# Moving two input loads and a weight load, with a new order of all work, in a linear-attention and mixer-MLP kernel

## The chip, the cores and the metric

The kernel runs on one core of one Trainium2 chip. A core has five engines that run side by side, each through its own list in order: TensorE (PE) multiplies, VectorE (DVE), ScalarE (ACT) and GpSimd (POOL) do element-wise work, and SyncE (SP) issues the DMAs here, apart from a few that ScalarE issues at the start. The metric is the time of one execution on the device in microseconds (us); less is better.

## The reference, cut to what matters

S = 2048 tokens of width D = 448; H = 16 heads of 28; MLP width 1792; all arrays are bf16.

```python
xn = layernorm(A_x)
# A: linear attention
q, k, v = heads(xn @ wqkv)
phi = lambda t: concat(softmax(t @ w_phi), softmax(-t @ w_phi))
kv, z = sum_s phi(k)^T v, sum_s phi(k)
A = (phi(q) kv / (phi(q) z + 1e-6)) @ wo
# B: token mixer and MLP, on xn
h  = gelu(layernorm(xn) @ w1)
x1 = xn + shift(h) @ w2        # four column blocks, shifted by +1, -1, +2, -2 tokens
B  = x1 + gelu(layernorm(x1) @ w3) @ w4
out = A_x + A + B
```

## The kernel before, in words

The tokens are cut into 16 tiles of 128. Every instruction is first recorded by a small class (`Recorder`, lines 19 to 222) together with the memory that it reads and writes; `solve` works out from the recorded order which instruction has to wait for which, and `emit` writes each engine's list. So the order in which the Python code calls things fixes two matters: the order within each engine's own list, SyncE's DMA issues among them, and who waits for whom. An instruction that waits holds up all that is behind it on its engine. Nearly all rows of a profile therefore carry the line of a helper: 204 a matmul, 208 a transpose on PE, 212 a ScalarE instruction, 216 one of VectorE or GpSimd, 219 a DMA transpose, 222 a plain DMA.

The loads at the start (lines 366 to 387) alternate between SyncE's queue and ScalarE's. `load_x(i, n)` brings n tiles of x into `xtok`; `load_half` brings half a weight. `load_wT` (line 381) transposes 112 rows' worth of the q (t = 0) or k (t = 1) weights by DMA into `wT`, whose memory is called `hi` in a profile; five such transposes are recorded before the order of the work begins. `load_w2` (line 389) loads w2 in three DMAs: 336 KB for three row blocks, and the last 64 rows twice, once for each half of the partitions.

The work comes in two lists, written out by hand.

The first list (lines 944 to 968) is handed to `chain` (line 561) and holds the jobs until the first products with w2. PE's rows are used in two halves, a lower and an upper one of 64 rows each, which run side by side; `chain` interleaves the steps of the two halves and holds the upper half of a product back by a lag of 400 columns. A string of digits says for each product which half takes four of its seven steps. The jobs are:

- `L(("m", i))`: the layer-norm statistics of tile i, two VectorE instructions. `L(("r", i, 1))`: the inverse root on GpSimd; `L(("q", i, 1))`: the same on ScalarE. `L(("a", i))`: normalise tile i into `xn` on VectorE; `L(("p", i))`: the same on GpSimd, behind a small negation.
- `XT(i, bank, n, engine)`: transpose n tiles on PE and copy them from PSUM to `xnT` on ScalarE, on VectorE or half on each ("2"). `XD(i)`: transpose tile i by a DMA.
- `ZV(i, EV(...))`: the V product of tile i (weight `wv`), and the engine that copies it out into `vaug`. `vb` and `gb` name the PSUM banks.
- `ZW`, `ZH`: the products with w1 for a group of four tiles, or half a group, and their GELU on ScalarE into `hT`. `ZR(h, bank)`: those for the last 64 columns of w1; their GELU goes to `hR`, and `rest_T(h)` transposes that by DMA into `hRT`. (In a profile hR has the name gT.)
- `FO`: folds the feature-map weights `w_phi` into the k or q weights (`wpk`, `wpq`). `phi_blocks` builds what the folds multiply with.
- `h_shift(g)`: six DMAs from `hT` to `hT` that move token columns for half of the tokens.
- `HD(bank, n)`: filler products on constants, whose result is not used.
- `HF(p, half)`: the halves of the first pair of k, w2 and q products; `HF(1, 0)` is the first one that reads w2, `hT` and `hRT`.

The second list (lines 1035 to 1059) holds the rest: k and q products and their exponentials (`k0`, `k1`, `q0`, `q1`), w2 products (`w0`, `w1_`), the k normalisation (`kn` on VectorE, `kx` on GpSimd), statistics of the second norm (`lo`), its scale (`sc`) and its application (`A` on GpSimd, `AD` on VectorE), DMA transposes (`T` of phi(q), `G` of the second norm's result), the sum over tokens (`K`), the w3 products (`a`, `b`), the attention output (`N`), the w4 and wo products (`f`) and the stores (`S`).

The name `w` in a profile stands for several tensors whose names are one letter and a digit, w1, w2, w3 and w4 among them.

Of the kernel before, what the change touches and what calls it, by code (L numbers as in the profile page):

```python
# [224 lines left out]
def bass_parallel_sum__linear_kernel_hedgehog__mixer_s_mlp__prompt_kernel(  # L225
    nc, A_x, A_wqkv, A_w_phi, A_wo, B_x, B_w1, B_w2, B_w3, B_w4, out,
):
    _, S, D = A_x.shape
# [14 lines left out]
    with es:  # L243
# [106 lines left out]
        def load_x(i, n, eng="SP"):  # L350
            R.dma(xtok[:, i:i + n, :], x2d[128 * i:128 * (i + n), :].rearrange("(j p) d -> p j d", p=128), eng)
# [9 lines left out]
        def load_half(dst, src, h, eng="SP"):  # L361
            R.dma(dst[:, 2 * h:2 * h + 2, :], src[192 * h:192 * h + 256, :].rearrange("(c p) d -> p c d", p=128), eng)
# [573 lines left out]
        def HF(p, n):  # L936
# [157 lines left out]
```

## Time and profile before

| | us |
|---|---|
| median of 3 runs | 171.0 (170.87 to 171.48) |
| the profiled execution | 171.11 |
| its span, from the first to the last instruction on the core | 169.4 |
| PE busy | 165.0 |
| VectorE busy | 109.9 |
| GpSimd busy | 92.4 |
| ScalarE busy | 79.6 |

The profile is one execution; its clock columns show TensorE granted its full clock (1.00) throughout. A matmul of a half-height tile overlaps one of the other half, so busy time of PE is not yet PE at its peak. "SPq" is SyncE's queue: a row there is the time that the issue of a DMA took, not its transfer. In a row of the timeline, the numbers are start and length in us, and a bracket at the end is the idle time of the engine before it, with what ended it. In a row of the groups, the numbers behind the bar are busy us and the mean in ns, and behind the second bar idle us. In a row of the DMA issues, the last number is the time from issue to landing.

### The profile page before, as it was taken

The page shows a single profiled execution, that of the slowest core. Times are in us where ns is not written, and L with a number is a line of the kernel's source. Part 1 is how long each engine was busy: PE and PEld are TensorE (multiplying, and loading weights), DVE is VectorE, ACT ScalarE, POOL GpSimd, SP SyncE. Part 2 cuts the span into 40 slices and gives each one's busy share as a digit, 9 for nine tenths or more (in the row PEclk, how much of TensorE's full clock was granted, in tenths as well). Part 3 has the DMA queues.
Part 4 walks back from the last instruction along what each step waited for, and adds up shares of the span by engine and source line. Part 5 has one row for each costly group of instructions (what it writes and reads, how often), then busy time and mean ns, then how long its engine had stood idle before and what let it go on. Part 6 is the DMA issues. An engine that isn't in the chain of part 4 may idle for free.

```text
span 169.4 us, 5416 instructions
## 1 busy us (share of the span) xinstructions
PE 165.0 (97%) x2355; PEld 99.2 (59%) x2355; DVE 109.9 (65%) x247; ACT 79.6 (47%) x107; POOL 92.4 (55%) x126
## 2 busy tenths in 40 slices
PE   8899999999999999999999999999999999999994
PEld 7476678666888775535554555545555555544453
DVE  2899777269999999995885836755755252560031
ACT  3489964849998787455242420440140222224000
POOL 5569872002999999994455684162362724252040
DMA  5995443799999976459785159363133112013021
GB/s 146 356 217 105 75 90 85 144 294 270 194 117 240 241 102 191 68 112 130 165 110 107 24 108 154 77 106 63 32 66 85 35 54 62 0 31 99 17 81 54
DMA packets 50583, 19.93 MB, mean 118 GB/s; under 512 B 41728, under 2 KB 49856, under 8 KB 50560
## 3 DMA queue, kind: packets, MB, share of 16 engines
q1 hardware_dynamic: 49440, 18.71, 55.1%
q10 hardware_dynamic: 1120, 0.89, 1.6%
q8 instruction: 18, 0.29, 0.8%
q14 instruction: 5, 0.04, 0.1%
HBM read 7.14 MB, written 1.84 MB: 53 GB/s over the span
## 4 chain that ended last, share of the span: by engine, by line
PE 86%; SPq 4%; DMA 4%; DVE 3%; POOL 1%; issue 1%
PE banks L204 85%; SPq L222 4%; DMA xtok<-in_A_x_dram 2%; DMA hRT<-gT 2%; DVE st L216 1%; PE banks L208 1%; DVE vaug L216 1%; POOL rs L216 1%; DVE mv L216 0%; POOL xn L216 0%; DVE xn L216 0%; SPq L219 0%
## 5 line engine op out<-in xcount | busy, mean ns | idle before, releaser
L212 ACT ACTIVATE phik<-banks 128x1024 bf16<-128x1024 f32 (+1 forms) x44 | 41.6, 987 | 63.5 <-PE banks L204 63.5
L204 PE MATMUL banks<-gT,w 64*128 64x512 bf16 x392 | 47.1, 376 | 0.1
L216 DVE TENSOR_TENSOR vaug<-banks,vaug 128x464 f32<-128x464 f32 (+3 forms) x65 | 32.8, 514 | 20.5 <-PE banks L204 18.8
L204 PE MATMUL banks<-w,phik 64*128 64x448 bf16 (+3 forms) x434 | 45.2, 343 | 0.0
L216 POOL TENSOR_TENSOR xnT<-vaug 128x280 bf16<-128x280 f32 (+1 forms) x32 | 18.1, 588 | 35.6 <-DVE vaug L216 35.6
L721 POOL TENSOR_TENSOR phik<-phik,rks 128x1792 bf16<-128x1792 bf16 x8 | 25.6, 3215 | 15.3 <-DVE rks L216 15.3
L204 PEld LDWEIGHTS banks<-w,phik 64*128 64x128 bf16 (+1 forms) x434 | 22.3, 94 | 19.5 <-issue 0.4
L204 PE MATMUL banks<-wv,xnT 64*128 64x448 bf16 (+2 forms) x222 | 33.0, 346 | 0.1
L204 PEld LDWEIGHTS banks<-gT,w 64*128 64x128 bf16 x392 | 18.3, 94 | 19.5 <-ACT phik L212 1.4
L216 POOL TENSOR_TENSOR vaug<-xn,xtok 128x448 f32<-128x448 bf16 x16 | 16.2, 1032 | 9.1 <-DVE vaug L216 9.1
L204 PEld LDWEIGHTS banks<-wv,xnT 64*128 64x128 bf16 (+1 forms) x222 | 13.7, 94 | 9.0 <-ACT xnT L212 0.8
L216 DVE RECIPROCAL vaug<-banks 128x16 f32<-128x16 f32 x16 | 4.1, 257 | 21.6 <-PE banks L204 21.6
L204 PE MATMUL banks<-xnT,w 64*128 64x512 bf16 (+1 forms) x105 | 17.6, 334 | 0.0
L216 DVE TENSOR_REDUCE ksum<-phik 128x64 f32<-128x1792 bf16 x8 | 16.0, 1997 | 0.2 <-ACT phik L212 0.2
L204 PE MATMUL banks<-wpk,xnT 64*128 64x448 bf16 x112 | 15.4, 349 | 0.0
L204 PE MATMUL banks<-wpq,xnT 64*128 64x448 bf16 x112 | 15.1, 349 | 0.0
L212 ACT ACTIVATE hi<-banks 128x896 bf16<-128x896 f32 x16 | 13.9, 937 | 1.2 <-PE banks L204 1.2
L204 PE MATMUL banks<-w,hT 64*128 64x448 bf16 x96 | 14.0, 349 | 0.0
L216 POOL TENSOR_TENSOR rs<-mv,mhalf 128x1 f32<-128x1 f32 (+1 forms) x14 | 9.6, 690 | 2.6 <-DVE mv L216 2.4
L216 POOL TENSOR_SCALAR g_tok<-xn,rs 128x512 bf16<-128x512 bf16 x12 | 9.2, 775 | 2.9 <-DMA gT<-g_tok 2.6
L204 PEld LDWEIGHTS banks<-wpk,xnT 64*128 64x128 bf16 x112 | 8.7, 94 | 2.6 <-ACT phik L212 0.2
L216 DVE BATCH_NORM_STATS2 st<-xtok 128x6 f32<-128x448 bf16 x16 | 9.7, 604 | 0.7 <-DMA xtok<-in_A_x_dram 0.7
(63 smaller groups left out, 167.2 us busy)
## 6 DMA issues: line engine op xcount, KB each, us to landing
w<-in_B_w_dram SPq DMA_DIRECT2D x2, 896.0 KB, 5.5
out_dram<-vaug SPq DMA_DIRECT2D x15, 112.0 KB, 1.9
w<-in_B_w_dram SPq DMA_DIRECT2D x2, 784.0 KB, 5.6
xtok<-in_A_x_dram SPq DMA_DIRECT2D x2, 448.0 KB, 6.5
wv<-in_A_wo_dram SPq DMA_DIRECT2D x2, 224.0 KB, 3.7
xtok<-in_A_x_dram SPq DMA_DIRECT2D x3, 112.0 KB, 4.0
xtok<-in_A_x_dram ACTq DMA_DIRECT2D x3, 112.0 KB, 4.2
w<-in_B_w_dram SPq DMA_DIRECT2D x1, 336.0 KB, 4.3
```

Of the source, the lines that this page charges most:

```text
L204: self.op("PE", lambda e: e.matmul(out, lhsT, rhs, start=start, stop=stop, skip_group_check=True), [out], [lhsT, rhs], tile=self._tile(lhsT))
L208: self.op("PE", lambda e: e.transpose(out, in_, ident), [out], [in_, ident], tile=self._tile(in_))
L212: self.op("ACT", lambda e: e.activation(out, in_, func, **kw), [out], [in_] + aps)
L216: self.op(eng, lambda e: getattr(e, name)(out, *args, **kw), [out], aps)
L222: self.op(eng, lambda e: e.dma_start(out, in_), [out], [in_], dma=True)
L721: R.op(pool, lambda e: e.tensor_tensor(ph, ph, wide, op=ALU.mult), [ph], [ph, wide, *after])
```

## The change

Four things are changed. The loads of x for tiles 2 and 3 stand ahead of those of wv. `load_w2` takes a part: part 0 is the 336 KB DMA, part 1 one DMA that brings the last 64 rows to both halves of the partitions, from a source that is read twice (a leading dimension of 2 with step 0); part 0 stands behind the V product of tile 2 and ahead of the last three `load_wT`, part 1 ahead of `phi_blocks`. Both lists are put in a new order, with other engines for some applications, roots and copies, other banks for some products and another string of digits. The statistics of the first norm are all `m` jobs, on VectorE, on both sides. The first norm has nine tiles applied on GpSimd and seven on VectorE on both sides, ten roots on GpSimd and six on ScalarE.

```diff
         load_x(0, 1)
         load_x(1, 1, "ACT")
+        load_x(2, 1)
+        load_x(3, 1, "ACT")
         load_half(wv, wv_d, 0)
         load_half(wv, wv_d, 1, "ACT")
-        load_x(2, 1)
-        load_x(3, 1, "ACT")
...
-        def load_w2(eng="SP"):
-            R.dma(w2[:, 0:NH, :], B_w2[0:REST, :].rearrange("(m p) d -> p m d", p=128), eng)
-            for h in range(2):
-                R.dma(w2[64 * h:64 * h + 64, NH, :], B_w2[REST:D, :], eng)
+        def load_w2(h, eng="SP"):
+            if h:
+                tail = B_w2[REST:D, :]
+                R.dma(w2[:, NH, :], bass.AP(tail.tensor, tail.offset, [[0, 2], *tail.ap]), eng)
+            else:
+                R.dma(w2[:, 0:NH, :], B_w2[0:REST, :].rearrange("(m p) d -> p m d", p=128), eng)
...
-        vb = {0: 6, 1: 7, 2: 5, 3: 0, 4: 6, 5: 5, 6: 1, 7: 1, 8: 0, 9: 7, 10: 6, 11: 2, 12: 7, 13: 7, 14: 5, 15: 2}
-        gb = ((4, 2, 3), (7, 6, 4), (3, 0, 5), (0, 5, 6))
+        vb = {0: 6, 1: 7, 2: 5, 3: 0, 4: 6, 5: 5, 6: 0, 7: 1, 8: 0, 9: 7, 10: 2, 11: 3, 12: 7, 13: 7, 14: 5, 15: 2}
+        gb = ((4, 2, 3), (7, 6, 4), (6, 0, 5), (0, 5, 6))
         spin(30)
         chain([
-            HD(1, 3), HD(3, 3), do(load_wT, 0, (1, 2, 3)), HD(2, 3), L(("m", 1)), L(("q", 1, 1)), L(("m", 0)),
-            L(("q", 0, 1)), HD(3, 3), L(("a", 1)), L(("p", 0)), HD(5, 3), XT(1, 2, 1, "ACT"), HD(0, 3), L(("m", 2)),
-            L(("m", 3)), XT(0, 2, 1, "ACT"), L(("q", 3, 1)), L(("r", 2, 1)), L(("m", 4)), L(("a", 3)), L(("q", 4, 1)),
-            L(("m", 5)), ZV(1, EV(1, "ACT", 1)), ZV(0, EV(0, "ACT", 1)), L(("p", 2)), XT(2, 4, 1, "ACT"),
-            inside(1, ZH(1, 0), XT(3, 0, 1, "ACT")), L(("m", 7)), L(("r", 5, 1)), L(("a", 4)), L(("p", 5)),
-            L(("q", 7, 1)), L(("m", 6)), L(("r", 6, 1)), ZH(2, 0), L(("a", 7)), ZV(2, EV(2, "ACT", 1)),
-            inside(1, ZH(0, 0), XT(4, 0, 1, "ACT")), L(("p", 6)), inside(2, ZH(0, 1, EW(0, 0, 1)), XT(5, 6, 1, "2")),
-            L(("m", 15)), inside(1, ZH(2, 1), XT(7, 0, 1, "2")), L(("q", 15, 1)), L(("p", 15)),
-            ZV(4, EV(4, "ACT", 1)), L(("m", 14)), inside(2, ZH(1, 1, EW(0, 1, 2)), XT(6, 0, 1, "DVE")), L(("m", 12)),
-            ZV(5, EV(5, "ACT", 1)), L(("r", 14, 1)), L(("m", 13)), L(("p", 14)), ZV(6, EV(6, "ACT", 1)), L(("m", 11)),
-            ZW(1, 0, EW(1, 0, 1)), ZW(1, 1, EW(1, 1, 1)), ZW(1, 2, EW(1, 2, 1)), L(("m", 10)), L(("r", 13, 1)),
-            L(("r", 12, 1)), XT(14, 2, 2, "ACT"), L(("a", 12)), L(("r", 11, 1)), ZV(7, EV(7, "DVE", 1)), L(("a", 13)),
-            L(("m", 8)), L(("p", 11)), ZV(3, EV(3, "ACT", 1)), ZV(15, EV(15, "ACT", 1)), XT(12, 6, 1, "2"),
-            do(kv_picks), XT(13, 3, 1, "2"), do(phi_blocks), L(("r", 10, 1)), L(("r", 8, 1)), XD(11),
-            L(("a", 10)), XD(10), ZV(14, EV(14, "ACT", 1)), L(("m", 9)), L(("p", 8)), ZV(12, EV(12, "DVE", 1)),
-            ZW(3, 0, EW(3, 0, 1)), XT(8, 3, 1, "ACT"), FO(1, 2, 0), do(h_shift, 0), L(("r", 9, 1)),
-            ZW(3, 2, EW(3, 2, 1)), FO(1, 0, 0), FO(1, 2, 1), ZV(13, EV(13, "ACT", 1)), ZW(3, 1, EW(3, 1, 1)),
-            FO(1, 0, 1), L(("p", 9)), ZV(8, EV(8, "DVE", 1)),
+            L(("m", 1)), L(("r", 1, 1)), L(("m", 0)), HD(1, 3), L(("q", 0, 1)), HD(6, 3), L(("p", 0)), HD(1, 3),
+            L(("a", 1)), L(("m", 2)), HD(5, 3), XT(1, 0, 1, "ACT"), HD(4, 3), L(("q", 2, 1)), HD(4, 3), L(("m", 3)),
+            L(("m", 4)), XT(0, 2, 1, "ACT"), L(("m", 5)), L(("q", 3, 1)), L(("p", 2)), ZV(1, EV(1, "ACT", 1)),
+            L(("p", 3)), L(("q", 4, 1)), ZV(0, EV(0, "ACT", 1)), L(("r", 5, 1)), L(("a", 4)), L(("m", 7)),
+            XT(2, 4, 1, "ACT"), ZH(2, 0), inside(1, ZH(1, 0), XT(3, 0, 1, "2")), L(("q", 7, 1)),
+            ZV(2, EV(2, "ACT", 1)), do(load_w2, 0), L(("m", 6)), L(("p", 5)), inside(1, ZH(0, 0), XT(4, 0, 1, "ACT")),
+            L(("q", 6, 1)), L(("p", 6)), L(("a", 7)), inside(2, ZH(0, 1, EW(0, 0, 1)), XT(5, 6, 1, "2")),
+            inside(1, ZH(2, 1), XT(7, 0, 1, "ACT")), L(("m", 15)), do(load_wT, 0, (1, 2, 3)), ZV(4, EV(4, "ACT", 1)),
+            L(("m", 14)), inside(2, ZH(1, 1, EW(0, 1, 2)), XT(6, 0, 1, "DVE")), ZV(5, EV(5, "ACT", 1)),
+            ZV(3, EV(3, "ACT", 1)), L(("m", 10)), L(("r", 14, 1)), ZW(1, 0, EW(1, 0, 1)), L(("a", 14)),
+            ZW(1, 1, EW(1, 1, 1)), L(("r", 15, 1)), L(("p", 15)), L(("r", 10, 1)), L(("m", 12)), L(("m", 8)),
+            ZW(1, 2, EW(1, 2, 1)), L(("m", 13)), L(("r", 12, 1)), XT(14, 2, 2, "DVE"), ZV(7, EV(7, "ACT", 1)),
+            ZV(6, EV(6, "ACT", 1)), L(("r", 13, 1)), L(("a", 12)), L(("m", 11)), L(("p", 13)),
+            ZV(15, EV(15, "DVE", 1)), XT(12, 6, 1, "DVE"), L(("a", 10)), XT(13, 3, 1, "ACT"), do(load_w2, 1),
+            do(phi_blocks), L(("r", 11, 1)), ZV(14, EV(14, "ACT", 1)), ZV(12, EV(12, "ACT", 1)), XD(10), L(("a", 11)),
+            L(("r", 8, 1)), XD(11), L(("m", 9)), L(("p", 8)), do(kv_picks), ZW(3, 0, EW(3, 0, 1)), XT(8, 3, 1, "ACT"),
+            FO(1, 2, 0), ZW(3, 2, EW(3, 2, 1)), FO(1, 0, 0), FO(1, 2, 1), ZV(13, EV(13, "ACT", 1)),
+            ZW(3, 1, EW(3, 1, 1)), FO(1, 0, 1), ZV(8, EV(8, "DVE", 1)), L(("r", 9, 1)), L(("p", 9)),
             inside(3, ZR(0, 6, (rest_out, 0, 6), (rest_T, 0)), XT(9, 1, 1, "DVE")), FO(0, 0, 0), FO(0, 2, 0),
-            ZR(1, 7, (rest_out, 1, 7)), do(load_w2), FO(0, 0, 1), ZW(2, 2, EW(2, 2, 1)), ZW(2, 1, EW(2, 1, 1)),
-            FO(0, 2, 1), do(load_w3, 0), ZV(10, EV(10, "ACT", 1)), ZW(2, 0, EW(2, 0, 1)), do(rest_T, 1),
-            ZV(9, EV(9, "ACT", 1)), ZV(11, EV(11, "DVE", 1)), HF(1, 0), HF(0, 0), HF(2, 0), HF(1, 1), do(late_3), do(kv_ones),
-            HF(0, 1), HF(2, 1), do(h_shift, 1)], 400,
-            "100100110101110000101010011110100")
+            do(late_3), do(h_shift, 0), ZR(1, 7, (rest_out, 1, 7)), FO(0, 0, 1), do(kv_ones), ZW(2, 2, EW(2, 2, 1)),
+            ZW(2, 1, EW(2, 1, 1)), ZW(2, 0, EW(2, 0, 1)), FO(0, 2, 1), do(load_w3, 0), ZV(11, EV(11, "ACT", 1)),
+            ZV(9, EV(9, "DVE", 1)), ZV(10, EV(10, "ACT", 1)), HF(1, 0), do(rest_T, 1), HF(0, 0), do(h_shift, 1),
+            HF(2, 0), HF(1, 1), HF(0, 1), HF(2, 1)], 400,
+            "010101010101101100001010011111000")
...
         play([
-            (lo, 1), (load_w3, 1), (k0, 1), (w0, 2), (lo, 0), (kn, 0), (k1, 1), (q0, 1), (w1_, 2), (q1, 1), (T, 0),
-            (k0, 2), (q0, 2), (k1, 2), (q1, 2), (k0, 3), (q0, 3), (T, 1), (kn, 1), (T, 3), (k1, 3), (w0, 4), (q1, 3),
-            (kx, 0), (kn, 2), (T, 2), (kx, 1), (w1_, 4), (kn, 3), (k0, 4), (T, 5), (w0, 6), (k1, 4), (lo, 3), (kx, 2),
-            (q0, 4), (lo, 2), (w1_, 6), (q1, 4), (kn, 4), (k0, 5), (kx, 3), (k0, 6), (sc, 0), (k1, 5), (w0, 8),
-            (wo_in,), (q0, 5), (A, 0), (w1_, 8), (k1, 6), (T, 6), (AD, 1), (T, 4), (q0, 6), (kn, 5), (T, 7), (q1, 5),
-            (w0, 10), (load_w4, 0), (A, 3), (k0, 7), (A, 2), (w1_, 10), (q1, 6), (lo, 5), (lo, 6), (w0, 12), (k1, 7),
-            (q0, 7), (G, 0), (K, 0), (kx, 4), (K, 1), (G, 1), (kx, 5), (lo, 7), (lo, 4), (G, 2), (K, 3), (K, 4),
-            (G, 3), (sc, 4), (K, 6), (A, 7), (kn, 6), (K, 9), (q1, 7), (load_w4, 1), (A, 6), (A, 4), (w1_, 12),
-            (K, 8), (K, 5), (K, 7), (lo, 10), (A, 5), (K, 11), (K, 2), (kx, 6), (G, 4), (kn, 7), (G, 7), (K, 10),
-            (a, 0), (lo, 11), (kx, 7), (a, 1), (G, 6), (b, 0), (lo, 12), (b, 1), (w0, 14), (a, 2), (lo, 8), (a, 3),
-            (lo, 9), (b, 2), (G, 5), (b, 3), (sc, 8), (w1_, 14), (T, 15), (a, 4), (a, 5), (b, 4), (b, 5), (T, 12),
-            (lo, 14), (K, 13), (lo, 15), (T, 10), (K, 15), (K, 14), (T, 14), (K, 12), (a, 6), (a, 7), (A, 9), (b, 6),
...
+            (k0, 1), (lo, 1), (w0, 2), (k1, 1), (lo, 0), (kn, 0), (q0, 1), (w1_, 2), (q1, 1), (kx, 0), (kn, 1),
+            (k0, 2), (q0, 2), (k1, 2), (k0, 3), (q1, 2), (load_w3, 1), (kx, 1), (T, 0), (q0, 3), (k1, 3), (T, 1),
+            (kn, 2), (w0, 4), (q1, 3), (w1_, 4), (kn, 3), (kx, 2), (k0, 4), (w0, 6), (k1, 4), (lo, 2), (q0, 4),
+            (T, 2), (w1_, 6), (kx, 3), (wo_in,), (T, 4), (q1, 4), (k0, 5), (lo, 3), (sc, 0), (k0, 6), (kn, 4),
+            (k1, 5), (A, 0), (T, 5), (T, 3), (w0, 8), (q0, 5), (w1_, 8), (AD, 1), (k1, 6), (T, 7), (q0, 6), (q1, 5),
+            (A, 3), (w0, 10), (T, 6), (load_w4, 1), (A, 2), (k0, 7), (G, 0), (kn, 5), (kx, 4), (w1_, 10), (kx, 5),
+            (lo, 5), (q1, 6), (w0, 12), (k1, 7), (G, 3), (lo, 6), (q0, 7), (K, 0), (lo, 4), (lo, 7), (K, 9), (K, 1),
+            (K, 2), (sc, 4), (K, 5), (G, 2), (K, 3), (G, 1), (kn, 6), (A, 5), (q1, 7), (w1_, 12), (K, 6), (AD, 4),
+            (K, 8), (load_w4, 0), (K, 4), (K, 11), (A, 6), (A, 7), (lo, 9), (K, 10), (G, 6), (lo, 10), (K, 7),
+            (kx, 6), (a, 0), (a, 1), (b, 0), (b, 1), (w0, 14), (kn, 7), (a, 2), (a, 3), (lo, 8), (b, 2), (kx, 7),
+            (b, 3), (w1_, 14), (a, 4), (lo, 12), (lo, 11), (sc, 8), (a, 5), (b, 4), (lo, 13), (b, 5), (lo, 14),
+            (G, 5), (G, 7), (K, 12), (K, 14), (K, 13), (K, 15), (a, 6), (G, 4), (kc,), (a, 7), (kb,), (T, 9),
...
```

More of the change, by code (lines that the diff above doesn't have):

```diff
@@ new lines, in bass_parallel_sum__linear_kernel_hedgehog__mixer_s_mlp__prompt_kernel @@
+            (lo, 15), (T, 13), (A, 11), (b, 6), (b, 7), (N, 0), (T, 11), (f, 1, 0), (N, 1), (a, 9), (a, 8), (AD, 8),
+            (G, 8), (b, 9), (AD, 10), (N, 2), (b, 8), (f, 2, 0), (a, 11), (N, 3), (a, 10), (T, 12), (G, 10), (A, 9),
+            (G, 9), (f, 3, 0), (b, 10), (b, 11), (f, 4, 0), (G, 11), (N, 5), (a, 12), (sc, 12), (a, 13), (f, 1, 1),
+            (f, 3, 1), (S, 0), (b, 13), (A, 13), (N, 4), (f, 2, 1), (N, 7), (b, 12), (f, 4, 1), (T, 8), (a, 15),
+            (a, 14), (S, 2), (b, 15), (N, 6), (T, 10), (b, 14), (A, 12), (f, 1, 2), (AD, 14), (a, 16), (A, 15),
@@ new lines, in bass_parallel_sum__linear_kernel_hedgehog__mixer_s_mlp__prompt_kernel @@
+            (a, 17), (G, 14), (S, 1), (b, 16), (S, 3), (b, 17), (G, 13), (T, 15), (f, 3, 2), (a, 18), (N, 9), (G, 12),
+            (f, 2, 2), (N, 8), (b, 18), (a, 19), (G, 15), (f, 4, 2), (b, 19), (N, 11), (a, 20), (f, 1, 3), (f, 3, 3),
+            (b, 20), (N, 13), (f, 2, 3), (f, 4, 3), (S, 5), (a, 21), (S, 7), (a, 22), (T, 14), (b, 21), (N, 10),
+            (b, 22), (f, 1, 4), (f, 3, 4), (a, 23), (S, 4), (N, 12), (f, 2, 4), (a, 24), (S, 6), (f, 4, 4), (b, 24),
+            (b, 23), (N, 15), (f, 1, 5), (S, 8), (a, 25), (N, 14), (f, 3, 5), (b, 25), (f, 2, 5), (a, 26), (f, 4, 5),
@@ L1060, in bass_parallel_sum__linear_kernel_hedgehog__mixer_s_mlp__prompt_kernel @@
+            (a, 27), (S, 10), (S, 11), (S, 9), (b, 26), (b, 27), (f, 1, 6), (f, 2, 6), (fin_tails,), (f, 3, 6),
+            (S, 13), (S, 12)])
         fin_full(14)
```

12 lines of the change are left out of this document (removed).

## The prediction, made before the changed kernel was run

> **What bounds the kernel now.** I read the page's busy table first, then the busy time by stage, then the chain that ended last, and only then the single rows at the places where these three disagree.
>
> ```profile
> span 169.4 us, 5416 instructions
> PE 165.0 (97%) x2355; PEld 99.2 (59%) x2355; DVE 109.9 (65%) x247; ACT 79.6 (47%) x107; POOL 92.4 (55%) x126
> ```
>
> TensorE (PE) is busy 97% of the span. The change removes no matmul: six groups of filler products (HD), 30 spins, the same V, w1, fold and head products, two tiles (10, 11) by DMA transpose, all stand on both sides of the diff, and each V or w1 product has seven of its eight half-height steps whichever way its digit points. So the time can only move where PE waits, or runs one half of its rows alone. The stages (columns: PE, PEld, DVE, ACT, POOL busy with counts, clock, DMA share, GB/s) show where that is:
>
> ```profile
> 5.70:13.00 7.30, 6.46 (x123) 4.20 (x118) 6.72 (x20) 5.32 (x15) 5.48 (x10) 1.00 1.25 265
> 32.00:36.00 4.00, 3.77 (x40) 2.09 (x41) 0.85 (x5) 2.40 (x3) 0.00 (x0) 1.00 0.80 223
> ```
>
> PE idles 0.84 us in 5.7 to 13 and 0.23 us in 32 to 36; behind that the chain below shows next to nothing. Two places remain: the start, where it waits for normalised tiles, and the join at 33 us, where the first product with w2 begins. The chain, in order of time, names the join:
>
> ```profile
> 30.12 2.72 DMA hRT<-gT
> 32.97 32.65 PE banks L204 x513
> 65.72 101.35 PE banks L204 x1269
> ```
>
> After the transpose into hRT lands, at 32.84, PE runs to the end practically without a gap. Whatever PE gains before 33 us is therefore kept, if the other engines move with it; whatever it loses is lost.
>
> **The change, part by part.**
>
> *w2 out of the queue ahead of hRT.* SyncE's queue (start, length, operation, count; the colon rows give shortest, median and longest in ns) is full from 5.48 on:
>
> ```profile
> 5.48 14.00 SPq L219 DMA_TRANSPOSE hi<-in_A_wqkv_dram  x8
> L219 SPq DMA_TRANSPOSE hi<-in_A_wqkv_dram x8: 1247/1260/3019, 5.5 to 18.2; - x8
> 19.52 3.49 SPq L219 DMA_TRANSPOSE xnT<-xn  x2
> 23.06 4.55 SPq L222 DMA_DIRECT2D hT<-hT  x6
> 27.65 2.43 SPq L222 DMA_DIRECT2D w<-in_B_w_dram  x3
> 30.12 1.27 SPq L219 DMA_TRANSPOSE hRT<-gT  x1
> L222 SPq DMA_DIRECT2D w<-in_B_w_dram x5: 542/589/1204, 27.6 to 37.2; - x5
> PEld banks L204 <- DMA w<-in_B_w_dram: 0.3, 1, 0.3
> ```
>
> Three w2 issues stand between the shift copies (hT) and the hRT transpose: 30.12 - 27.65 = 2.47 us. Two issues come in their place, one ahead of the last three wT transposes, one ahead of the two xnT transposes: 2 x 0.65 (the median 0.589 and a step to the next) = 1.3 us. So all from the xnT transposes on starts 1.3 us later, and hRT starts at 30.12 - 2.47 + 1.30 = 28.95 and lands 2.72 us on, at 31.67, 1.17 us earlier. What PE did there:
>
> ```profile
> 32.40 0.35 PE L204 MATMUL banks<-wv,xnT 64*128 64x448 bf16 x1
> 32.97 0.35 PE L204 MATMUL banks<-w,hRT 64*128 64x448 bf16 x1 [0.23 <-DMA hRT<-gT]
> 33.16 0.35 PE L204 MATMUL banks<-wpk,xnT 64*128 64x448 bf16 x1
> 33.37 0.35 PE L204 MATMUL banks<-w,hT 64*128 64x448 bf16 x1
> 32.59 0.55 ACT L212 ACTIVATE vaug<-banks 128x448 bf16<-128x448 f32 x1
> 33.56 0.62 DVE L216 CAST vaug<-banks 128x448 bf16<-128x448 f32 x1 [3.37 <-PE banks L204]
> hT<-hT SPq DMA_DIRECT2D x1, 95.8 KB, 4.0
> ```
>
> Ordinary starts are 0.19 us apart (32.97 to 33.16); 32.40 to 32.97 is 0.57, so the stall is **0.38 us**. What is late next? First bank 7: the K product (wpk) may start only when ScalarE has copied V of tile 9 out, at 32.59 + 0.55 = 33.14, just before it did start. Without hRT's stall this would give the 0.38 back; but the change moves that copy to VectorE, which idles 3.37 us there, and takes bank 6 from V of tile 10 to the w1 product, evicted earlier. Next the last shift copy: issued at 27.02 (27.61 less 0.59), landed 4.0 on, at 31.0; 1.3 later is 32.3. The upper half reads it at 33.37 in this run, at about 32.5 when PE comes 0.88 earlier: a cover of 0.2 us. I take 0.38; bounds 0 (shift copies take the place of hRT) and 0.38. The shift copies stand later in the list than they did, but in SyncE's own order still between the xnT transposes and hRT. What the two w2 issues push back has cover:
>
> ```profile
> 26.28 0.48 PE L204 MATMUL banks<-g_tok,hi 48*128 48x56 bf16 x16
> hi<-in_A_wqkv_dram SPq DMA_TRANSPOSE x8, 4.7
> xnT<-xn SPq DMA_TRANSPOSE x2, 3.5
> 27.46 0.38 PE L204 MATMUL banks<-xnT,w 64*128 64x512 bf16 x1
> ```
>
> The last wT issue starts at 18.2 and is down near 23 by the median of 4.7; the fold that reads it is the first row. The xnT transposes, issued from 19.52 to 23.01 and down 3.5 after their starts, have landed near 25; after the change near 26.3, against a reader at 27.46 - 0.88 = 26.6: covered by 0.3.
>
> [...]
>
> *x of tiles 2 and 3 ahead of wv; root of tile 2 on ScalarE, tile 3 on GpSimd, tiles 4 and 5 earlier.* The start, on VectorE, GpSimd and PE:
>
> ```profile
> 5.77 0.63 DVE L216 BATCH_NORM_STATS2 st<-xtok 128x6 f32<-128x448 bf16 x1 [0.31 <-DMA xtok<-in_A_x_dram]
> 6.71 0.57 POOL L216 TENSOR_TENSOR rs<-mv,mhalf 128x1 f32<-128x1 f32 x1
> 7.66 0.77 POOL L216 TENSOR_SCALAR xn<-xtok,rs 128x512 bf16<-128x512 bf16 x1
> 9.98 0.37 DVE L216 TENSOR_SCALAR xn<-xtok,mv,rs 128x512 bf16<-128x512 bf16 x1
> 10.50 0.77 POOL L216 TENSOR_SCALAR xn<-xtok,rs 128x512 bf16<-128x512 bf16 x1
> 6.64 0.29 PE L208 MATMUL banks<-ident,xn 64*128 64x64 bf16 x8 [0.61 <-POOL xn L216]
> wv<-in_A_wqkv_dram SPq DMA_DIRECT2D x1, 224.0 KB, 3.9
> L212 ACT ACTIVATE rs<-mv 128x1 f32<-128x1 f32 x6 | 1.2, 203 | 3.4 <-DVE mv L216 3.4
> ```
>
> VectorE waits 0.31 us for x of tile 2; with it there, statistics start behind tile 1's apply (0.1 later than now, since tile 1's root goes through GpSimd), 0.2 us earlier. A root on ScalarE (the last row, 0.20 us) instead of 0.57 on GpSimd brings tile 2's normalised rows from 8.43 to about 7.9; tile 4's apply moves ahead of tile 7's statistics, from 9.98 to about 8.5, and tile 5's from 10.50 to about 9.9; tile 3's, now the third in GpSimd's row, comes a little later than VectorE made it, with one more w1 half-product ahead of it on PE. Tile 0, whose wait of 0.61 is the longest, does not move. wv, issued 0.47 later behind one more x on each queue, lands near 5.7 instead of 5.1; its first product ran at 6.75, a cover of one microsecond. What it is worth:
>
> ```profile
> L204 PE MATMUL banks<-wv,xnT 64*128 64x448 bf16 x25 | 5.1, 350 | 0.1
> L204 PE MATMUL banks<-xnT,w 64*128 64x256 bf16 x36 | 4.4, 270 | 0.0
> L208 PE MATMUL banks<-ident,xn 64*128 64x64 bf16 x56 | 2.0, 192 | 0.7 <-POOL xn L216 0.6
> ```
>
> With both halves of its rows running, a 448-column step costs 0.094 us (half of 0.19), so this window's work is 25 x 0.094 + 36 x 0.054 + 56 x 0.013 = 5.0 us of 7.3. Of the 2.3 us lost, about 1.3 lies before tile 0's eviction ends near 7.6 and stays. Bounds 0 and 1.0; I take half, **0.5 us**, because four of the six tiles come earlier and one later.
>
> *All statistics on VectorE.* Sixteen "m" jobs stand on both sides; nothing moves in this part: 0.
>
> *Everything behind 36 us.* The head of the list for PE keeps its order but for two neighbours. Three moves deserve a price. The transpose of q for tile 3 goes behind wo's two loads and two others, to an issue near 50 and a landing near 54; its reader's successor on ScalarE overwrites the rows at 58.06. Tile 4's apply goes from GpSimd to VectorE, with one more statistics pair ahead of the last k normalisation:
>
> ```profile
> 70.40 0.55 DVE L216 RECIPROCAL rks<-ksum 128x64 f32<-128x64 f32 x1
> 69.09 6.39 POOL L721 TENSOR_TENSOR phik<-phik,rks 128x1792 bf16<-128x1792 bf16 x2
> 76.34 0.69 PE L204 MATMUL banks<-phik,vaug 128*30 128x64 bf16 x64
> ```
>
> The reciprocal ends at 70.95, some 1.15 us later after the change, at 72.1; GpSimd could begin that last product only at 72.3, and ends at 75.48, 0.86 us ahead of its reader. Cost 0, bounds -0.3 and +0.4 for the unseen rest. The early loads of the w4 halves trade places, both many microseconds ahead of use.
>
> **Sum.** 0.38 + 0.50 = 0.88 us off the profiled 171.11 (span 169.4 and 1.71 around it) gives 170.23; that run lies 0.11 above the median of 171.0, so on the median **170.1**.
>
> **Rivals.**
> 1. *More of the start is won:* all 1.0 us, the stall's 0.38 and 0.3 behind: 171.0 - 1.7 = 169.3. For it speaks that PE keeps what it gains; against, that VectorE is busy 6.72 of 7.30 us there and still has all statistics to do.
> 2. *The shift copies take hRT's place:* they land 1.3 us later than now, 32.3 plus whatever the queue adds; if it adds half a microsecond or more, PE starts the upper half no earlier than today and the early gain is waited away: about 170.9.
> 3. *The two w2 parts hold the queue up (slower):* the first of the eight wT issues took 3.02 us against 1.26 for the usual one, with loads ahead of it. Let c be what each part costs the queue; I counted 0.65. The last shift copy then lands at 31.0 + 2c, and PE needs it by 33.37 to be no worse than now: c = 1.2 decides. With a long issue like that behind each part, c = 0.65 + 1.76 = 2.4, it lands at 35.8, 2.4 us too late: 173.4; slower than 0.5% needs c over 1.6.
> 4. *The tail part goes over two engines:* at 265 GB/s over 16, two carry 33 GB/s, and 112 KB take 3.5 us instead of 0.4, ahead of the xnT transposes on those two. They would land at 26.3 + 3.1 = 29.4 at worst, against a reader at 26.6; of these 2.8 us I take 2, since their own issue of 3.49 us runs meanwhile: 171.0 - 0.9 + 2 = 172.1, if a transpose waits for every engine. [...]
> 5. *The change does not do what it says:* true of the statistics already; price 0, within the forecast.
>
> **Chances.** About 0.5% is what a measurement of this kernel can tell from no change: 170.15 to 171.85. The forecast 0.50, half of it on either side of 170.15 (0.27 and 0.23); rival 1 0.15; rival 2 0.15; rival 3 0.12; rival 4 0.08. Faster 0.27 + 0.15 = 0.42; same 0.23 + 0.15 = 0.38; slower 0.20. The range runs from rival 1's 169.3 to 172.0, leaving out the far part of rivals 3 and 4 (some 0.15) and little below.
>
> **What would show it.** Right: no wait for hRT or w2 on PE's rows near 32; the first wpk product at 32.2 to 32.4 instead of 33.16; tiles 2, 4, 5 transposed earlier; SyncE's hRT issue near 29. Wrong: the first product with hT waits for a shift copy; a SyncE issue of over 2 us behind a w2 part; the first w1 product of tiles 8 to 11 waits for xnT; or new PE gaps behind 36 us, where I looked at three moves of some two hundred.

## The result and the profile after

| | before | after |
|---|---|---|
| median, us (9 runs each, side by side) | 170.87 (170.43 to 171.48) | 173.4 (171.69 to 175.37) |
| ratio | | 1.0106, 95% interval 1.0077 to 1.0134 |
| profiled execution, us | 171.11 | 174.97 |
| its span, us | 169.4 | 173.2 |

The kernel became slower; 170.1 was forecast, in a range of 169.3 to 172.0. The ratio leaves out three of the nine runs, which were the longest and had a lower TensorE clock; the experiments below show that this low clock belongs mostly to the change, so the median tells more than the ratio.

The page of the changed kernel: span, busy table, and the granted clock in 40 slices.

```profile
span 173.2 us, 5408 instructions
PE 166.7 (96%) x2355; PEld 104.8 (61%) x2355; DVE 110.5 (64%) x248; ACT 78.9 (46%) x105; POOL 91.7 (53%) x125
PEclk9999999699999999999999999999999999999999
```

PE is 1.7 us busier with the same 2355 matmuls, and one slice, the eighth (30 to 35 us), has a 6 where the others have a 9: something there ran at a lower clock. The chain that ended last names the place.

```profile
22.63 6.67 DMA xnT<-xn
29.30 0.04 issue
29.35 40.10 PE banks L204 x642
69.45 0.10 issue
69.55 101.35 PE banks L204 x1269
```

hRT, the link of the chain before, is gone. In its place stands a transpose into xnT that takes 6.67 us. The last row is the measuring stick for all that follows: from the first w3 product TensorE runs 101.35 us to its end, before and after alike. It began at 65.72 before and at 69.55 now, 3.83 later; the spans differ by 3.8. So in this execution nothing was won or lost behind that product, and the stages ahead of it must hold it all (columns as before: PE, PEld, DVE, ACT, POOL busy, clock, DMA share, GB/s):

```profile
5.70:13.00 7.30, 6.77 (x139) 5.14 (x135) 6.36 (x19) 5.79 (x16) 5.18 (x10) 1.00 1.38 284
20.00:26.00 6.00, 6.00 (x129) 4.37 (x126) 4.59 (x12) 4.33 (x8) 4.59 (x8) 1.00 1.05 62
26.00:29.50 3.50, 0.75 (x33) 0.52 (x27) 0.62 (x1) 0.00 (x0) 0.60 (x2) 1.00 1.15 113
29.50:32.00 2.50, 2.50 (x86) 2.50 (x82) 1.19 (x3) 0.60 (x1) 0.00 (x0) 0.55 0.49 67
32.00:36.00 4.00, 4.00 (x54) 3.25 (x52) 1.22 (x3) 2.10 (x4) 0.00 (x0) 0.86 0.56 112
```

The start did get better (6.77 us busy of 7.30, against 6.46). Then PE stands still for 2.75 of 3.5 us, and in the 6.5 us behind it runs for a while at a reduced clock, which by these rows costs 2.5 x 0.45 + 4.0 x 0.14 = 1.7 us. Two rows set at the points where the clock changes show one stretch of 3.41 us at 0.50, and PE busy for only 0.66 of the 3.41 us ahead of it:

```profile
26.34:29.75 3.41, 0.66 (x31) 0.50 (x30) 0.32 (x1) 0.00 (x0) 0.26 (x1) 1.00 1.26 126
29.75:33.16 3.41, 3.41 (x85) 3.23 (x78) 1.32 (x5) 0.84 (x2) 0.00 (x0) 0.50 0.29 41
```

2.75 + 1.7 less 3.83 leaves a lead of 0.6 us that was won elsewhere in these stages. The second row of the table, 20 to 26 us, points to the cause: 62 GB/s at a DMA share above 1. Little moves, and much is queued. SyncE's queue, and the PE rows that wait:

```profile
20.55 0.74 SPq L222 DMA_DIRECT2D w<-in_B_w_dram  x1
21.35 2.74 SPq L219 DMA_TRANSPOSE xnT<-xn  x2
31.83 1.21 SPq L219 DMA_TRANSPOSE hRT<-gT  x1
```

```profile
28.81 0.20 PE L204 MATMUL banks<-w,xnT 64*128 64x64 bf16 x2 [2.41 <-DMA xnT<-xn]
29.35 1.07 PE L204 MATMUL banks<-w,xnT 64*128 64x64 bf16 x43 [0.34 <-DMA xnT<-xn]
30.50 0.63 PE L204 MATMUL banks<-xnT,w 64*128 64x512 bf16 x1
```

The tail of w2, the one DMA with a source read twice, is issued at 20.55, and the two transposes of tiles 10 and 11 right behind it. Here is what the DMA engines moved from 22 to 26 us, in 40 slices of 0.1 us, and the issues of 20 to 31 us (the last number is us to landing):

```profile
GB/s 18 36 0 0 0 15 132 223 236 224 189 177 215 5 0 9 36 45 54 18 18 20 0 0 18 54 36 54 54 36 54 54 36 54 54 36 54 54 36 54
```

```profile
xnT<-xn SPq DMA_TRANSPOSE x2, 7.0
hT<-hT SPq DMA_DIRECT2D x1, 63.9 KB, 5.8
```

The transposes took 7.0 us instead of 3.5, and a shift copy 5.8 instead of 3.1. In the last 1.5 us of the slices 36 and 54 GB/s alternate: a trickle of some 48 GB/s, against 177 to 236 in the burst before. The same view of these 1.5 us alone:

```profile
DMA packets 80, 0.07 MB, mean 48 GB/s; under 512 B 0, under 2 KB 80, under 8 KB 80
q1 hardware_dynamic: 80, 0.07, 13.7%
```

0.07 MB in 80 packets fits 896 bytes each, which is one row of w2, and 13.7% of 16 engines is 2.2. So the trickle is the tail of w2, on about two DMA engines.

### The profile page after: what moved, and what is told of

Same layout as the page of the kernel before. It is cut to its first block, busy times and chain, and to the rows that moved or that the text cites. A ratio compares the mean times of both kernels' runs of the same rounds, so it can differ in the third digit from the quotient of the medians.

```text
span 173.2 us, 5408 instructions
## 1 busy us (share of the span) xinstructions
PE 166.7 (96%) x2355; PEld 104.8 (61%) x2355; DVE 110.5 (64%) x248; ACT 78.9 (46%) x105; POOL 91.7 (53%) x125
## 4 chain that ended last, share of the span: by engine, by line
PE 90%; DMA 7%; SPq 1%; issue 0%; DVE 0%
PE banks L204 89%; DMA xnT<-xn 4%; DMA w<-in_B_w_dram 3%; SPq L222 1%; PE banks L208 1%; DVE vaug L216 0%
## 5 line engine op out<-in xcount | busy, mean ns | idle before, releaser
L216 POOL TENSOR_TENSOR xnT<-vaug 128x196 bf16<-128x196 f32 (+1 forms) x32 | 18.2, 589 | 37.0 <-DVE vaug L216 37.0
L204 PEld LDWEIGHTS banks<-wv,xnT 64*128 64x128 bf16 (+1 forms) x222 | 14.2, 94 | 7.9 <-ACT xnT L212 0.4
L204 PE MATMUL banks<-xnT,w 64*128 64x512 bf16 (+1 forms) x105 | 18.4, 352 | 0.3 <-DMA w<-in_B_w_dram 0.3
L216 DVE TENSOR_TENSOR xn<-banks,xn 128x512 bf16<-128x512 f32 (+1 forms) x16 | 8.9, 600 | 2.7 <-PE banks L204 2.6
L204 PEld LDWEIGHTS banks<-wpk,xnT 64*128 64x128 bf16 x112 | 9.3, 94 | 1.5 <-ACT phik L212 0.2
```

Of the source, the lines that this page charges most:

```text
L204: self.op("PE", lambda e: e.matmul(out, lhsT, rhs, start=start, stop=stop, skip_group_check=True), [out], [lhsT, rhs], tile=self._tile(lhsT))
L216: self.op(eng, lambda e: getattr(e, name)(out, *args, **kw), [out], aps)
```

## The experiments

The theory at the outset: the tail of w2 goes over few DMA engines and holds the transposes behind it (rival 4); the rest of the change does what was forecast. Rivals: the moved x loads and the order lose the time, or the clock differs by itself. All ratios are to the kernel before, run on the same chip beside it.

**The tail as two DMAs**

```diff
-                R.dma(w2[:, NH, :], bass.AP(tail.tensor, tail.offset, [[0, 2], *tail.ap]), eng)
+                for s in range(2):
+                    R.dma(w2[64 * s:64 * s + 64, NH, :], tail, eng)
```

> The changed kernel with the last 64 rows of w2 loaded by two DMAs of 64 partitions each, as the kernel before does, in the changed kernel's place. Theory (the one DMA with a source that is read twice runs on about two DMA engines and holds up the two xnT transposes behind it): the second xnT transpose lands near 26 instead of 29.3, PE has no wait for xnT of over 0.5 us, and the time is 170.0 to 170.6, 0.3 to 0.9 us below the kernel before. Rival (any w2 part ahead of the transposes costs the queue, whatever its shape): one issue more, so xnT lands at 29.5 or later and the time is that of the changed kernel, about 172.5, or 0.6 more.

171.25 us, ratio 0.9997 (0.9973 to 1.002). The loss is gone by this edit alone, and no run of 12 listed a clock below 0.999. But the kernel before isn't beaten, and the time is above the 170.6 that the theory allowed. The waits of this kernel:

```profile
26.71 0.81 PE L204 MATMUL banks<-w,xnT 64*128 64x64 bf16 x43 [0.43 <-DMA xnT<-xn]
33.09 0.35 PE L204 MATMUL banks<-w,hRT 64*128 64x448 bf16 x1 [0.34 <-DMA hRT<-gT]
```

Two DMAs fill SyncE's queue longer than one (1.23 us against 0.74), so the transposes into xnT and hRT still come a little late, and the stall at hRT that the change was to remove is back.

**Only the tail changed, in the kernel before**

```diff
-            for h in range(2):
-                R.dma(w2[64 * h:64 * h + 64, NH, :], B_w2[REST:D, :], eng)
+            tail = B_w2[REST:D, :]
+            R.dma(w2[:, NH, :], bass.AP(tail.tensor, tail.offset, [[0, 2], *tail.ap]), eng)
```

> The kernel before with nothing changed but the last 64 rows of w2: one DMA with the source read twice, in the place of the two DMAs, ahead of the hRT transpose. Theory: the transpose into hRT waits behind it on its engines and lands 2 to 4 us later, near 35 to 36; PE waits for it; 172.5 to 174.5. Rival (the shape of the DMA costs nothing): one issue less, hRT lands 0.6 to 1.2 us earlier and the time is 170.3 to 170.9.

172.38 us, ratio 1.0078 (1.0049 to 1.0106). One edit of the form of a DMA, in the old place and order, costs 1.3 us by the ratio (1.1 by the medians):

```profile
33.31 0.36 PE L204 MATMUL banks<-w,hT 64*128 64x448 bf16 x1 [1.26 <-DMA w<-in_B_w_dram]
```

PE idles 1.26 us for w2 itself, and not for hRT, as I had expected; the time is just below the band of 172.5 to 174.5. With the first experiment this shows the cause from both sides.

**The same single DMA, earlier**

```diff
-... XT(13, 3, 1, "ACT"), do(load_w2, 1),
+... XT(13, 3, 1, "ACT"),
...
-            ZV(2, EV(2, "ACT", 1)), do(load_w2, 0), L(("m", 6)), ...
+            ZV(2, EV(2, "ACT", 1)), do(load_w2, 0), do(load_w2, 1), L(("m", 6)), ...
```

> The changed kernel with the one DMA of the last 64 rows moved directly behind the larger part of w2, ahead of the last three wT transposes. Theory: it is now those transposes that wait; the last lands 2 to 3 us later, near 24.5 to 25.5, still ahead of the folds that read it near 26, and xnT lands near 26: PE waits 0 to 1 us and the time is 170.2 to 171.2. Rival (w2 parts ahead of the xnT transposes cost the queue, or the new order of the work itself is slow): no gain, 172 to 173.

170.97 us, ratio 0.9995 (0.9964 to 1.0026). The slow DMA, now issued near 16 instead of at 20.55, hurts no one: no wait for xnT or hRT (PE is busy 10.00 of the 10 us from 26 to 36), and the first w3 product starts at 64.81, 0.91 us ahead of the kernel before; the forecast was 0.88. And yet the time is that of the kernel before. The lead is lost again here:

```profile
64.81 2.98 PE L204 MATMUL banks<-gT,w 64*128 64x512 bf16 x26
68.36 0.39 PE L204 MATMUL banks<-gT,w 64*128 64x512 bf16 x2 [0.57 <-issue]
```

PE stops for 0.57 us between two products that wait for nothing ("issue"). The first experiment has the same stop, shorter (0.29). Before, 28 products run through.

**Only x of tiles 2 and 3 ahead of wv, in the kernel before**

```diff
+        load_x(2, 1)
+        load_x(3, 1, "ACT")
         load_half(wv, wv_d, 0)
         load_half(wv, wv_d, 1, "ACT")
-        load_x(2, 1)
-        load_x(3, 1, "ACT")
```

> The kernel before with nothing changed but the loads of x for tiles 2 and 3 ahead of those of wv. By the prediction's step VectorE starts the statistics of tile 2 up to 0.3 us earlier and wv stays hidden: 0 to 0.3 us faster, 170.6 to 170.9. Rival (wv and w1, which landed 1.3 and 0.8 us later in the changed kernel's trace, become the late ones): PE waits for w1 near 8.7 and the time is 0.2 to 0.6 us longer, 171.1 to 171.5.

171.19 us, ratio 1.0002 (0.9977 to 1.0028): alone, that part is worth nothing.

**Filling the wait, first try**

```diff
+        def fill(n):
+            for _ in range(n):
+                R.mm(banks[5][:, 0:128], busy, busy, True, True)
...
-            ... ZR(1, 7, (rest_out, 1, 7)), ...
+            ... do(fill, 44), ZR(1, 7, (rest_out, 1, 7)), ...
```

> The changed kernel with 44 filler matmuls of 128x128 on a free bank right ahead of the first product that reads tiles 10 and 11, so that TensorE works while it waits for their transposes. Theory (the 2.4 us of idleness there cost a second time, because TensorE's clock was granted at 0.55 and then 0.86 in the 6.5 us that follow): the transposes land as late as before, near 28.8 and 29.3, but the clock stays at 1.00 and no run is above 173; all lie at 172.0 to 172.8. Rival (the granted clock has nothing to do with the idle time, it differs from run to run whatever TensorE does): runs still scatter from 171.7 to 175.4, and the profile shows a stretch below 1.00 behind 29 us.

178.6 us in three runs and 618.9 in one, which is the one profiled. There every product of 512 columns took 1101 ns on the mean, at a listed clock of 1.00:

```profile
L204 PE MATMUL banks<-gT,w 64*128 64x512 bf16 x392 | 168.5, 1101 | 0.0
```

It doesn't tell the theories apart: of the three runs at 178.6, two listed a clock of 0.99 in spite of the fillers. Neither time is explained. A very long run isn't peculiar to the fillers, though: the kernel before took 978.21 us in one of its runs beside the first four experiments, also at a listed 1.00.

**Filling the wait with half-height products**

```diff
+        def hold_w1(b, n):
+            return [[(banks[b + k][:, 0:448], busy[r, :], w1[r, 0, :], True) for _ in range(n)]
+                    for k, r in enumerate((slice(0, 64), slice(64, 128)))]
...
-            ... ZR(1, 7, (rest_out, 1, 7)), ...
+            ... ("both", hold_w1(4, 13), ()), ZR(1, 7, (rest_out, 1, 7)), ...
```

> The changed kernel with 26 filler products of 64 rows and 448 columns, in pairs, right ahead of the first product that reads tiles 10 and 11: 26 x 0.094 = 2.4 us of work that fills the wait. They replace the 128-row fillers of the earlier experiment, which took 178.6 for reasons not seen. Theory (idleness brings the clock down): the transposes land near 28.8 and 29.3 as before, the clock stays at 1.00 in 29.5 to 36 us, and all runs lie at 171.7 to 172.8. Rival (the clock does not depend on the idle time): a stretch below 1.00 behind 29 us all the same, and runs from 171.7 up to 175.

174.45 us (173.91 to 174.94), ratio 1.0201 (1.0163 to 1.0239). The times lie where the rival had them, but not for its reason. The wait is filled, and the clock stays at 1.00 behind it (all four runs list 1.00):

```profile
26.19 2.63 PE L204 MATMUL banks<-w,const-bfloat16-1.0 64*128 64x448 bf16 x26
28.66 1.05 PE L204 MATMUL banks<-w,xnT 64*128 64x64 bf16 x47
```

```profile
29.50:32.00 2.50, 2.50 (x88) 2.10 (x82) 1.32 (x5) 1.30 (x3) 0.00 (x0) 1.00 0.24 36
32.00:36.00 4.00, 4.00 (x45) 2.69 (x43) 1.72 (x2) 2.75 (x6) 0.00 (x0) 1.00 0.82 221
```

And the rest of the time went into the stop of the third experiment, four times as long:

```profile
69.53 0.60 PE L204 MATMUL banks<-gT,w 64*128 64x512 bf16 x4 [2.18 <-issue]
```

If all four runs had this stop, they would lie at 171.7 to 172.8 without its 2.18, as expected of full clock; only one was traced.

**The changed kernel once more**

> The changed kernel once more, beside the three that follow. Theory (its 173.4 is made of 2.4 us of waiting for the transposes of tiles 10 and 11, less the 0.9 won before, and of a clock that drops behind the wait, by different amounts from run to run): the wait is again 2.2 to 2.6 us in the trace; where the page shows no clock below 1.0 behind 29 us the time is 171.7 to 172.5, where it does it is 173.4 to 175.4. Rival (the spread has another cause, such as the start): a run near 172 with a low clock at 29 to 36 us, or one above 174 without.

174.33 us, ratio 1.0187 (1.0144 to 1.023). The profiled one, 173.12, kept its clock, after waits of 0.36, 1.71 and 0.41 us:

```profile
28.46 0.20 PE L204 MATMUL banks<-w,xnT 64*128 64x64 bf16 x2 [1.71 <-DMA xnT<-xn]
29.50:32.00 2.50, 2.50 (x97) 2.08 (x91) 1.31 (x5) 1.19 (x2) 0.00 (x0) 1.00 0.34 46
32.00:36.00 4.00, 4.00 (x50) 2.75 (x44) 1.72 (x2) 2.76 (x5) 0.00 (x0) 1.00 0.76 199
67.70 2.55 PE L204 MATMUL banks<-gT,w 64*128 64x512 bf16 x22
```

Its first w3 product comes at 67.70, 1.98 after that of the kernel before: this is the price at full clock. The time lies 0.6 above the band that was expected at full clock. The wait is as long as expected, 2.48 in sum (0.36 of it for a transpose of wT), but 2.48 less 1.98 leaves a lead of only 0.5, where the expectation took off 0.9. Over the 13 runs of the changed kernel, the six at full clock took 171.69 to 173.40 and the seven at 0.99 took 173.94 to 175.37; of the 83 runs of the kernel before in these comparisons none was below 0.999, nor any of the four with the wait filled by half-height products. Of the 102 runs of the nine kernels below and above that keep TensorE busy there or nearly so, six were at 0.99, and so were two of the three with 128-row fillers at 178.6. So with the long wait a lowered clock is listed in about half of the executions (7 of 13, of which one was traced) and seldom otherwise (6 of 102); four runs with the wait filled are few, and the trace of one of them is the stronger evidence.

**The stop at 68 us: where it comes from**

A page lists queues of their own for instructions, the larger of them q8. First its row in the kernel before, then the queues of the kernel with the early tail in two windows, 63.0 to 65.6 and 65.6 to 67.2 us (packets, MB, share of 16 engines):

```profile
q8 instruction: 18, 0.29, 0.8%
```

```profile
q1 hardware_dynamic: 852, 0.76, 99.0%
```

```profile
q1 hardware_dynamic: 38, 0.03, 5.8%
q8 instruction: 1, 0.02, 4.4%
```

18 transfers for 4710 matmuls and weight loads: one for each 260 or so, which is why I take q8 for TensorE's. While the second part of w4 (784 KB, issued at 61.58) fills the engines to 99%, no instructions come; as it ends, they do, from 65.90 to 67.04 (4.4% of 16 engines in 1.6 us is one transfer of 1.13 us). TensorE goes on at 68.36, 1.32 us after. In the filled one a transfer of q8 takes 5.5% of 16 engines from 67.0 to 68.3, which puts the arrival at 68.20; the restart is at 69.53, 1.33 after. In the first experiment the restart is at 68.98. The three stop at the same instruction, though not at the same product. The stretches from 0 to just before the restart, one row for each (early tail; tail in two; filled wait):

```profile
0.00:68.35 68.35, 66.21 (x1111) 49.88 (x1111) 55.91 (x112) 52.28 (x78) 45.88 (x67) 1.00 0.87 178
```

```profile
0.00:68.97 68.97, 66.25 (x1111) 49.11 (x1111) 55.67 (x111) 52.01 (x78) 45.61 (x67) 1.00 0.82 176
```

```profile
0.00:69.51 69.51, 66.27 (x1111) 49.92 (x1111) 54.46 (x110) 51.35 (x77) 44.33 (x66) 1.00 0.87 174
```

1111 matmuls and 1111 weight loads each time. The 26 fillers are 52 instructions, so there the stop comes 52 instructions earlier in the program, ahead of the first w3 product instead of behind the 26th. No order of products can do that; a block of instructions that ends there can. By q8's row above a transfer brings 16 KB (0.29 MB in 18) for those 260. No view names the instructions in it, so that a block ends there is what I conclude from the equal counts.

**The second load of w4 moved behind the next transposes**, in the kernel with the early tail

```diff
-            (K, 8), (load_w4, 0), (K, 4), ...
+            (K, 8), (K, 4), ...
-            (b, 3), (w1_, 14), (a, 4), ...
+            (b, 3), (w1_, 14), (load_w4, 0), (a, 4), ...
```

> The kernel with the tail of w2 directly behind its first part (171.0), and the second load of w4 (784 KB) moved behind the next four gT transposes, from 61.6 to about 73 us. Theory (TensorE's stop of 0.94 us at 67.4 is its next 16 KB of instructions, which were asked for at about 63.3 and came only at 65.9 to 67.0, behind that load): the instruction transfer starts near 63.5, the stop is gone, the lead of 0.84 us on the kernel before is kept, and the time is 170.1 to 170.4. Rival (the stop belongs to the order of the K products, or to an engine that the trace does not name): the stop stays at the same instruction, 171.0. Second rival (the lead is given back further on whatever happens at 68 us): no stop, and still 171.0.

171.93 us (170.62 to 174.18), ratio 1.0016 (0.9983 to 1.0048). No stop: 28 w3 products run through. The time didn't follow, for a reason at the other end, seen in this row and in those of the x loads below:

```profile
7.61 1.53 PE L204 MATMUL banks<-wv,xnT 64*128 64x448 bf16 x9 [0.85 <-ACT rs L212]
```

The first V product, at 6.75 in the kernel before, starts at 7.61, when wv has just landed (near 7.5). (The row names ScalarE's root, which ended at 6.51.)

**The changed first list with the second list of the kernel before**, and the tail of w2 early, as above:

> The changed kernel's loads and first list with the tail of w2 directly behind its first part, and from 36 us on the second list of the kernel before. Theory (the change's start is worth 0.84 us, and its second list loses it at 68 us because the load of w4 there ends later against TensorE than in the kernel before): the second list of before leaves 1.3 us between the arrival of the instructions and their use, so the 0.84 us are kept: 170.1 to 170.5. Rival (any run that is ahead by 0.8 us loses it, because other engines set the pace behind 64 us): 171.0.

170.69 us, ratio 0.9979 (0.9942 to 1.0017), its first w3 product at 65.07 and no stop behind it: in the profiled execution the lead of 0.65 is kept, to a time of 170.49. But 5 of 12 runs took over 171.3, and the median lies between the two theories.

**The x loads in their old order**: the kernel with the late w4 load, the one with the old second list, and the one with the early tail alone, each with

```diff
-        load_x(2, 1)
-        load_x(3, 1, "ACT")
         load_half(wv, wv_d, 0)
         load_half(wv, wv_d, 1, "ACT")
+        load_x(2, 1)
+        load_x(3, 1, "ACT")
```

> The same kernel as the one with the late second load of w4, but with x of tiles 2 and 3 loaded behind wv again. Theory (the start was worth some 0.5 us, and x of tiles 2 and 3 is the larger part of it, because the new list normalises them earlier): tile 2's transposes come 0.3 to 0.5 us later, TensorE is 0.3 to 0.5 us less ahead at 35 us, and the time is 170.5 to 170.8. Rival (the order of the x loads is worth nothing, as it was in the kernel before): within 0.1 of the kernel it is compared with, TensorE's row at 35 us too.

> The first list of the change with the tail of w2 directly behind its first part, x of tiles 2 and 3 behind wv as in the kernel before, and the second list of the kernel before. Theory (the lead of 0.8 us comes from the new first list and from w2 out of hRT's way, not from the order of the x loads, and the second list of before does not lose it): 170.0 to 170.5, TensorE 0.8 us ahead of the kernel before at 35 us and at the end of the span. Rival (the x loads carry the lead): 170.8 to 171.2.

> As the kernel that ran at 170.56 (old order of the x loads, second load of w4 late), but with the second load of w4 back in the change's place, at about 61.6 us. Nothing else differs. Theory (the 16 KB of instructions that TensorE asks for near 63.3 queue behind those 784 KB): the instruction transfer starts near 65.9 instead of 63.5, TensorE stops for 0.6 to 1.0 us near 67.5 at the same instruction as in the two kernels that stopped there, and the time is 171.0 to 171.4. Rival (the load of w4 has no part in it): no stop, 170.4 to 170.7.

| | x ahead of wv | x behind wv |
|---|---|---|
| early tail, w4 late | 171.93, 1.0016 (0.9983 to 1.0048) | 170.56, 0.9961 (0.9926 to 0.9995) |
| early tail, second list of before | 170.69, 0.9979 (0.9942 to 1.0017) | 169.92, 0.9942 (0.9912 to 0.9973) |
| early tail | 170.97, 0.9995 (0.9964 to 1.0026) | 170.19, 0.9958 (0.9938 to 0.9979) |

Three pairs, and in each the old order is better by 0.4 to 0.6%. (The first pair ran on one chip; the other two are compared over the kernel before.) The intervals of each pair overlap, so it is the three together that speak for the old order. Of the first pair I had expected the opposite; its 170.56 lies in the expected band by luck, since its partner came out at 171.93. The second kernel agrees with its theory (169.92 against 170.0 to 170.5), and the third came nearer to its rival. The issue of wv with its time to landing, in the kernel before, in the changed kernel's second profile, and in the one with the late w4 load:

```profile
wv<-in_A_wqkv_dram SPq DMA_DIRECT2D x1, 224.0 KB, 3.9
```

```profile
wv<-in_A_wqkv_dram SPq DMA_DIRECT2D x1, 224.0 KB, 4.9
```

```profile
wv<-in_A_wqkv_dram SPq DMA_DIRECT2D x1, 224.0 KB, 5.8
```

With x in front, wv is issued 0.45 later and also takes 0.8 (in the changed kernel's first profile) to 1.9 us longer, so it lands 1.3 to 2.4 us later.

The last kernel is a miss: the stop that I expected didn't come (first row), and the time is better than both theories had it.

```profile
64.51 3.20 PE L204 MATMUL banks<-gT,w 64*128 64x512 bf16 x28
5.70:13.00 7.30, 6.92 (x143) 5.27 (x145) 6.96 (x21) 6.00 (x16) 5.20 (x11) 1.00 1.26 258
```

The transfer of its instructions starts at 63.10, ahead of the bulk of w4, whose issue came at 61.99 instead of 61.58; so they passed. That is no argument against my reading of the stop, but by it the stop hangs on a race of a few tenths of a microsecond (0.41 between the two issues).

The version with both old pieces, at 169.92, has the lowest median here: 0.6% below the kernel before.

## Why the prediction was wrong, point by point

**w2 out of the queue ahead of hRT (0.38 us): right in mechanism, but its cover was wrong.** With the tail out of the way there is no stall at hRT (the early tail: PE busy 4.00 of the 4 us from 32 to 36). The step that failed is the sentence "covered by 0.3" for the xnT transposes, on two counts. The reader is the products with the last columns of w1 (in the rows above, `banks<-w,xnT 64x64`), for which the kernel before is ready at 26.58, as its row shows, not the row at 27.46 that I named; and the landing "near 26.3" took a transpose's 3.5 us from a time when nothing slow stood ahead of it, where it took 7.0. One lands at 28.8, the other at 29.3.

```profile
26.58 0.80 PE L204 MATMUL banks<-w,xnT 64*128 64x64 bf16 x42
```

**Rival 4 was the true one, at a chance of 0.08.** Its bound, "29.4 at worst", is near the measured 29.30, and its 172.1 lies inside the 171.69 to 173.40 of the runs at full clock. That it fits so closely is partly luck: it assumes a tail at 33 GB/s, a wait of 2 us and a lead of 0.9, where 48 GB/s, 2.75 and 0.6 were measured. That the tail goes over two engines was an assumption: no row of the trace before splits a transfer by engine. What was run bears it out: the one DMA with the source read twice trickles at 48 GB/s in the changed kernel, with 13.7% of 16 engines, about two, in 24.5 to 26 us, and costs 1.3 us in the kernel before by itself; as two DMAs of 64 rows each, in the changed kernel's place, it lands in 2.7 us, and the xnT transposes behind it take 4.2 us where they took 7.0. That no row spoke for or against it was reason for an even chance, not for 0.08.

**What no rival had: the clock.** I priced a wait at its length. This one costs up to 1.7 us again, and takes the median from 172.5, that of the six runs at full clock, to 173.4. That rival 3 names this very 173.4 is luck: the two parts delayed the xnT issues by 1.83 us (from 19.52 to 21.35), a little over the 1.30 that I had counted and far from the 4.8 that its price needs.

**The start (0.5 us): about right in sum, wrong in its parts.** The new order of roots and applications is worth the gain: with the old x order, PE is busy 6.92 of 7.30 us there and reaches the first w3 product 1.2 us earlier than before. The moved x loads lose some 0.6 to 0.9 us of it on the median. The step that failed is that wv "lands near 5.7 instead of 5.1", with "a cover of one microsecond": I added the 0.47 us of a later issue, and left out that wv's own transfer gets longer behind the x loads (3.9 us from issue to landing before, 4.7 to 5.8 then). It landed at 6.4 in the changed kernel, still ahead of its reader there, and at 7.5 with the late w4, where PE waited.

**Statistics (0):** not tried alone; nothing in the traces speaks against it.

**Behind 36 us (0, bounds -0.3 and +0.4): right for the changed kernel, where 101.35 us follow the first w3 product as before, and wrong for the sum.** TensorE arrived there late. With the early tail it arrives 0.91 early, as I had forecast, and the stop for instructions takes 0.7 of it (0.2 are left at the end of the span). "Whatever PE gains before 33 us is therefore kept" was too simple.

What stays open: why the clock falls in some executions of the same wait and not in others (no run here fixes it), and why six runs of the other kernels were at 0.99 too, whose profiled executions have no wait of over 1.3 us; what the 128-row fillers did.

## What to carry to other kernels

Folding two DMAs into one saves issue time (0.74 us in SyncE's queue here against 1.23), but look at the transfer too: the one DMA with the source read twice moved at 48 GB/s on about two of 16 engines, and the transposes issued behind it took 7.0 us instead of 3.5. When an early gain doesn't reach the end, look for a stop that no semaphore explains and count the instructions up to it: here it stood behind the same 1111 matmuls and 1111 weight loads in three variants, which speaks against the order of the products and for the instructions, with a load of 784 KB under way ahead of them. Moving a load of 112 KB ahead of one of 224 KB, on each of two queues, cost the large one more than the time of an issue: 0.45 us of a later issue and 0.8 to 1.9 us of a longer transfer. So its reader's cover must be worked out from a landing under that traffic.

## What the runs showed of the hardware that I had not expected

- TensorE's clock was granted at 0.50 for one stretch of 3.41 us, behind 3.41 us in which it had been idle for 2.75 (two waits with 0.66 us of work around them); with 2.48 us of idleness in three pieces, in another execution, it stayed at 1.00. What sets the length of the stretch, no run here shows.
- TensorE stopped for 0.29, 0.57 and 2.18 us in three kernels, each time behind 1111 matmuls and 1111 weight loads, with no wait that the profile shows. I take it to have waited for its own instructions: in the two of these kernels whose windows show a transfer of q8 there, it went on 1.32 and 1.33 us after the arrival. In the kernel with the early tail and the old x order, where the transfer comes ahead of the bulk of w4, it starts at the 1976th matmul or weight load (987 and 989 by then, at 63.10 us), and what comes in it is, by this reading, needed behind the 2222nd. In the stretch of the K products 192 of them take 0.95 us, and from 63.10 us to the end of the 26th w3 product (64.51 + 2.98) are only 4.4 us, against 9.4 from one transfer to the next on the mean of the kernel before (169.4 us, 18 transfers).
